# Attention beside an FFT filter: matrix-engine work in longer runs of one tiling mode, two activation sets of two banks, another load order

## The chip, the cores and the metric

The kernel runs on one core of a Trainium2 chip. A core has a matrix engine (TensorE, PE in the profile) that writes into PSUM, eight banks of 128 partitions by 512 f32; a scalar engine (ACT), a vector engine (DVE) and GpSimd (POOL) that work on SBUF (ACT and DVE read PSUM too); and SyncE (SP), which here issues the DMA transfers. Each engine takes its own instructions in program order and waits on semaphores. The metric is the device time of one execution in microseconds; less is better.

## The reference

Two independent parts share the output, side by side.

```python
def _A_ref(x, w_r, w_i):              # x: 1 x 2048 x 640
    X = rfft2(x.astype(float32))      # over rows and columns
    X = X * (w_r + 1j * w_i)          # 2048 x 321 weights
    return irfft2(X, s=(2048, 640)).astype(bfloat16)

def _B_ref(x, wqkv, wo):              # x: 1 x 2048 x 640, 32 heads of 20
    qkv = (x @ wqkv).reshape(B, S, 3, 32, 20).transpose(2, 0, 3, 1, 4)
    q, k, v = qkv
    p = softmax(einsum("bhqd,bhkd->bhqk", q, k) * 20 ** -0.5)
    o = einsum("bhqk,bhkd->bhqd", p, v)
    return o.transpose(0, 2, 1, 3).reshape(B, S, 640) @ wo

return concatenate([a, b], axis=-1)   # 1 x 2048 x 1280 bfloat16
```

Part B is called the attention here, part A the filter.

## The kernel before, in words

**Attention.** The 32 heads are stored four to a group `g` (eight groups), each head in its own 32 partitions of `KT` and `QT`. A unit is one block of 512 queries and one group; there are 32 units. A unit has 64 score tiles: 16 blocks of 128 keys times 4 heads `j`. A score tile is one matmul of 32 rows by 128 columns with 512 moving columns into one PSUM bank (`score_mm`, L751). Matmuls of different `j` use different rows of the array and run beside each other; those of one such bundle are called a wave here. For the exponential a tile takes one of two ways. On ACT, L1247 makes the exponential of a set of banks: sets of three banks (0, 1, 2) and of two banks (3, 4) by turns, into rings of three buffers each. On DVE, one tile at a time goes from a bank to int16 (L875), and for four tiles together three operations (L903, L904, L905) make two f16 parts whose products are summed. The products with V are matmuls of 128 rows by 32 columns (L982, `try_pv`), one per ACT tile and two per DVE tile, of which four with different `j` can form a wave; they accumulate over a unit in one bank. A unit ends with a copy (L1003), four f32 matmuls that put queries into rows (L1015), a reciprocal and a product (L1022, L1028). When a query block has all eight groups, `jobs_out` transposes (L1050) and multiplies with `wo` (L1065).

**Full-array work.** All else on PE uses the array as 128 by 128: transposes of `x` (L533), the projections of the first two groups straight into place (`proj0`, L555), packed projections of the others (L581) whose rows DMAs on the chip then spread to the heads' partitions (`spread_heads`), V (L627), and the filter's four stages (L1464, L1515, L1601, L1627). The filter's input is folded on POOL (L1437 to L1445) after both halves were loaded into a zone that held `x`; its tables are loaded between stages into zones that earlier stages have left. Banks 5, 6 and 7 are shared by DVE tiles, V products and full-array work.

**Who sets the order.** A planner in the program (`run`, `step_pe`) simulates the engines with a table of durations and writes down each engine's instructions in the order in which it took them; `add` and `plan` then put in the semaphore waits. So the order is fixed when the program is built. On PE it takes, when free: a fill of an ACT set with score tiles (with at most one DVE tile beside it), else a DVE tile, else a wave of V products, else full-array work whose release time (`rel`, spread evenly over `FT0` to `FT1` for the filter) has come. SP takes the first DMA of its list whose inputs are there.

**The start.** SP loads `x` for the attention, then 16 narrow slices of `wqkv` for the first two groups (`pad_w`), then twelve broadcasts of constant rows into the spare partitions of `KT` and `QT` (`constR`), then the three thirds of `wqkv`.

## Time and profile before

| | |
|---|---|
| runs | 1002.26, 992.9, 996.78 us; median 996.78 us |
| profiled execution | 998.17 us; span of its instructions 996.4 us |
| mean granted TensorE clock | 0.944 of full |
| PE busy | 931.4 us, 93% |
| ACT busy | 792.8 us, 80% |
| DVE busy | 706.5 us, 71% |
| POOL busy | 84.6 us, 8% |
| ACT exponentials (L1247) | 331 of three banks, 335 of two, 3 of one |
| DVE tiles (L875) | 382 |

Busy shares are averages over the span. PE's matmuls overlap, so that a busy PE need not be one at its peak: what a matmul costs in a stream is read from the distance between starts, not from its own duration. The granted clock is given for each stretch of time; at 0.50 a matmul takes twice as long.

### The profile page before, as it was taken

Reading aid. Unit: us, or ns where it says so; the run is one execution under the profiler, and the core shown is the slowest. Engines: PE = TensorE matmul, PEld = TensorE weight load, DVE = VectorE, ACT = ScalarE, POOL = GpSimd, SP = SyncE. Lnnn points to the kernel's source line nnn. Section 1 sums busy time; section 2 is a strip of 40 time slices with the busy share of each in tenths; the row PEclk is TensorE's granted clock in tenths of the full one; section 3 lists DMA queues with packets and bytes.
Section 4 is the critical chain, followed back from the end, with each engine's and each line's share of the span. In section 5 each row is a group of like instructions: output and inputs, shape, how many; then the busy total and the mean of one; then the engine's idle time right before and its main releaser. Section 6 shows DMA issues by size and latency. Waiting matters only on the chain.

```text
span 996.4 us, 14901 instructions
## 1 busy us (share of the span) xinstructions
PE 931.4 (93%) x6322; PEld 321.6 (32%) x6372; DVE 706.5 (71%) x1082; ACT 792.8 (80%) x679; POOL 84.6 (8%) x93
## 2 busy tenths in 40 slices
PE   7479999999889999999999999999999999999997
PEld 3133422434222333223223333332333332333333
DVE  4427566687886877778737788785777776778874
ACT  3258487988875889889979898997888988888882
POOL 1000000000399100000020020100000000000000
PEclk9789999999765999999979999997999999999999
DMA  7940201110500001100110100011001000010001
GB/s 145 95 125 5 48 22 43 22 22 22 190 1 1 21 7 43 43 2 1 47 27 8 34 20 21 21 43 43 23 21 43 20 8 1 1 49 19 27 28 55
DMA packets 29697, 35.33 MB, mean 35 GB/s; under 512 B 13240, under 2 KB 26298, under 8 KB 28602
## 3 DMA queue, kind: packets, MB, share of 16 engines
q1 hardware_dynamic: 28858, 33.02, 13.2%
q0 software_dynamic: 768, 1.32, 0.5%
q8 instruction: 51, 0.84, 0.3%
q14 instruction: 20, 0.16, 0.1%
HBM read 24.66 MB, written 5.24 MB: 30 GB/s over the span
## 4 chain that ended last, share of the span: by engine, by line
PE 81%; DVE 9%; DMA 4%; ACT 2%; SPq 2%; issue 1%
PE ps L751 26%; PE ps L982 26%; PE ps L1601 5%; PE ps L1015 4%; PE ps L1464 4%; PE ps L581 4%; DVE arena L875 4%; DMA arena<-in_B_wqkv_dram 4%; PE ps L1627 3%; PE ps L1515 3%; PE ps L1065 3%; ACT arena L1247 2%; PE ps L627 2%; DVE arena L904 2%; SPq L421 2%
## 5 line engine op out<-in xcount | busy, mean ns | idle before, releaser
L1247 ACT ACTIVATE arena<-ps 128x1024 f16<-128x1024 f32 (+1 forms) x669 | 785.6, 1233 | 171.3 <-PE ps L751 139.6
L875 DVE TENSOR_SCALAR arena<-ps 128x512 int16<-128x512 f32 x382 | 260.2, 689 | 187.2 <-PE ps L751 184.3
L751 PE MATMUL ps<-arena 32*128 32x512 bf16 x2048 | 345.9, 399 | 15.5 <-ACT arena L1247 8.2
L982 PE MATMUL ps<-arena 128*32 128x512 f16 x2430 | 348.5, 404 | 7.2 <-DVE arena L904 3.3
L751 PEld LDWEIGHTS ps<-arena 32*128 32x128 bf16 x2048 | 81.8, 91 | 249.4 <-issue 133.5
L982 PEld LDWEIGHTS ps<-arena 128*32 128x32 bf16 x2430 | 81.1, 94 | 205.7 <-issue 174.6
L904 DVE TENSOR_TENSOR arena<-arena 128x2048 f16<-128x2048 f16 (+1 forms) x97 | 121.6, 1254 | 2.3
L903 DVE TENSOR_SCALAR arena<-arena 128x2048 uint16<-128x2048 uint16 (+1 forms) x97 | 69.4, 715 | 2.3
L905 DVE TENSOR_SCALAR arena<-arena 128x2048 uint16<-128x2048 uint16 (+1 forms) x97 | 66.9, 690 | 0.3
L1601 PE MATMUL ps<-arena 128*128 128x512 bf16 (+1 forms) x176 | 56.1, 394 | 1.3 <-issue 1.3
L1015 PE MATMUL ps<-arena 128*128 128x85 f32 x256 | 51.8, 315 | 1.5 <-DVE arena L1003 1.2
L627 PE MATMUL ps<-arena 128*128 128x160 bf16 x320 | 31.6, 240 | 20.9 <-DMA arena<-in_B_wqkv_dram 20.8
L581 PE MATMUL ps<-arena 128*128 128x512 bf16 x164 | 47.3, 383 | 2.4 <-issue 1.3
L1015 PEld LDWEIGHTS ps<-arena 128*128 128x128 f32 x256 | 38.2, 205 | 25.8 <-issue 16.1
L1464 PE MATMUL ps<-arena 128*128 128x512 bf16 x144 | 44.3, 384 | 2.0 <-issue 1.8
L1515 PE MATMUL ps<-arena 128*128 128x322 bf16 (+1 forms) x198 | 40.3, 309 | 2.0 <-DVE arena L875 0.6
L633 DVE CAST arena<-ps 128x320 bf16<-128x320 f32 x32 | 15.7, 492 | 34.3 <-PE ps L627 34.1
L1627 PE MATMUL ps<-arena 128*128 128x320 bf16 (+1 forms) x192 | 36.6, 302 | 0.6 <-DVE arena L875 0.2
L588 DVE TENSOR_SCALAR arena<-ps 128x512 bf16<-128x512 f32 x36 | 24.8, 689 | 16.5 <-PE ps L581 15.3
L1437 POOL TENSOR_TENSOR arena<-arena 128x640 f32<-128x640 bf16 x8 | 12.9, 1606 | 261.8 <-DMA arena<-in_A_x_dram 261.3
L1065 PE MATMUL ps<-arena 128*128 128x320 bf16 x160 | 32.1, 312 | 1.6 <-DMA out_dram<-arena 1.2
L627 PEld LDWEIGHTS ps<-arena 128*128 128x128 bf16 x320 | 22.2, 100 | 32.9 <-issue 30.4
(60 smaller groups left out, 399.7 us busy)
## 6 DMA issues: line engine op xcount, KB each, us to landing
arena<-ct SPq DMA_DIRECT2D x8, 1024.0 KB
out_dram<-arena SPq DMA_DIRECT2D x32, 160.0 KB
arena<-arena SPq DMA_DIRECT2D x42, 80.0 KB
arena<-in_A_x_dram SPq DMA_DIRECT2D x2, 1280.0 KB
arena<-in_B_wqkv_dram SPq DMA_DIRECT2D x3, 800.0 KB
arena<-constR SPq DMA_DIRECT2D x8, 288.0 KB
arena<-in_B_x_dram SPq DMA_DIRECT2D x3, 640.0 KB
arena<-cFD SPq DMA_DIRECT2D x1, 966.0 KB
```

What stands on the lines that cost most here:

```text
L581: return lambda e: e.matmul(o, l, r_, start=(cc == 0), stop=(cc == 4))
L627: return lambda e: e.matmul(o, l, r_, start=st, stop=(c == 4), skip_group_check=True)
L751: return e.matmul(self.ps[:, bank, :], self.KT[32 * j:32 * j + 32, g, kt * 128:(kt + 1) * 128], self.QT[32 * j:32 * j + 32, g, qc * 512:(q ...
L875: return e.tensor_scalar(o, in_, 0.0, 31744.0, ALU.max, ALU.min)
L903: (lambda e, en: e.tensor_scalar(Gu, Iu, 0x3FF, 0x3800, ALU.bitwise_and, ALU.bitwise_or), 70 + 0.26 * 512 * n, ik, [("G", b), ("G2", b)], ...
L904: (lambda e, en: e.tensor_tensor(Gf, If, Gf, ALU.mult), 70 + 0.52 * 512 * n, ik + [("G", b)], [("G2", b)], [], "p3"),
L982: inst = e.matmul(self.ps[32 * j:32 * j + 32, bank, :], v_, p_, start=s_, stop=False, tile_position=(0, 32 * j), skip_group_check=True)
L1015: return lambda e: e.matmul(o, l, self.sel, start=(qt == 0), stop=(qt == 3), skip_group_check=True)
L1247: self.put("act", lambda e: e.activation(o, in_, AF.Exp, bias=ACT_BIAS, scale=ACT_SCALE), 0.8333 * 512 * n + 95.0, r=[("ps", b) for b in b ...
L1464: return lambda e: e.matmul(o, l, r_, start=(t == 0), stop=(t == 7))
L1515: return lambda e: e.matmul(o, lhs, r_, start=st, stop=sp)
L1601: return lambda e: e.matmul(o, l, r_, start=(n == 0), stop=(n == 7))
```

## The change

- **Fewer, longer runs on PE.** The planner charges `SW` for each step between score matmuls ("S"), V products ("V") and full-array work ("B"). V products are taken when eight are ready (`VMIN`), up to four waves in one go, each wave made of different `j` (`pv_waves`). Work other than a fill is taken only as far as it fits before the next fill is due (`room`). A fill of an ACT set can bring up to two DVE tiles with it, all of different `j`; DVE tiles have no other way in.
- **Banks.** ACT sets are banks 0, 1 and 2, 3; banks 4 to 7 are shared. The exponentials go into one ring of seven buffers of two tiles. Up to three DVE tiles may be under way (two before), none before a planned time of 30 us.
- **Order of units.** `UNITS` takes query blocks 0 and 1 of groups 0 to 3 by turns, then the rest. `proj0` makes a second query block.
- **Loads.** The narrow slices are gone: two slices of 160 columns are loaded and four copies on DVE pad them. The constant rows are gone: 14 memsets on POOL fill `KT` and `QT`, and the spread transfers then overwrite the heads' rows. V's third of `wqkv` is loaded after the first half of `x`.
- **Fold.** The filter's input is loaded in rows of 128 right after the transposes of `x`, folded on POOL as before, stored to a scratch in DRAM, and loaded folded when the filter begins.
- The planner's durations and latencies have new values, and the last output copies may run on ACT.

The core of the diff:

```diff
+UNITS = ([(qc, g) for g in range(4) for qc in range(2)] + [(0, g) for g in range(4, 8)] + [(1, g) for g in range(4, 8)]
+         + [(qc, g) for qc in range(2, 4) for g in range(8)])
...
-    L_PE = 150.0
-    L_ACT = 120.0
...
+    L_PE = 215.0
+    L_ACT = 165.0
...
+    SW = 102.0
+    FILL = 445.0
+    SETS = ((0, 1), (2, 3))
+    POOLB = (4, 5, 6, 7)
+    RING = (7,)
...
+        self.dma(self.ident, cBd.ap()[:, 0:128], 32768, w=[("ident",)], name="ld_id")
+        for t in range(2):
+            self.dma(self.xn[0][:, 2 * t:2 * t + 2, :], xB[:, 2 * t:2 * t + 2, :], 327680, w=[("xn", 0, 2 * t), ("xn", 0, 2 * t + 1)], name="ld_x0")
+        for c0, nm in ((640, "wk0"), (0, "wq0")):
+            self.dma(self.wqkv[:, :, c0:c0 + 160], wv[:, :, c0:c0 + 160], 204800, w=[(nm,)], name="ld_" + nm)
...
+        def ld_x(i):
+            self.dma(self.xn[i], xB[:, 4 * i:4 * i + 4, :], 655360, w=[("xn", i, t) for t in range(4)], name="ld_x%d" % i)
+        ld_x(1)
+        self.dma(self.wqkv[:, :, 1280:1920], wv[:, :, 1280:1920], 819200, w=[("wv",)], name="ld_wv")
+        ld_x(2)
+        ld_x(3)
+        self.dma(self.wqkv[:, :, 800:1280], wv[:, :, 800:1280], 614400, w=[("wk",)], name="ld_wk")
...
-        crk = cRd.ap()[0:12, :].rearrange("p (g s) -> p g s", g=1).to_broadcast([12, 6, 2048])
-        crq = cRd.ap()[12:24, :].rearrange("p (g s) -> p g s", g=1).to_broadcast([12, 6, 2048])
...
-            p0, p1 = 32 * j + 20, 32 * j + 32
-            self.dma(self.KT[p0:p1, 2:8, :], crk, 294912, w=[("KTc", j)], name="ld_kc", rel=6000.0)
-            self.dma(self.QT[p0:p1, 2:8, :], crq, 294912, w=[("QTc", j)], name="ld_qc", rel=6000.0)
...
+                d_ = self.w0[g][i].rearrange("p c (j e) -> p c j e", e=32)[:, :, :, 0:20]
+                s_ = self.wqkv[:, :, 640 * i + 80 * g: 640 * i + 80 * g + 80].rearrange("p c (j e) -> p c j e", e=20)
+                self.dve_push([((lambda d_, s_: lambda e, en: e.tensor_copy(d_, s_))(d_, s_), 420.0, [("w0z",), (("wq0", "wk0")[i],)], [("w0", g, i)], [], "padw")],
...
+        for g in range(2, 8):
+            self.pool_op((lambda v: lambda e: e.memset(v, one2))(self.KT[:, g, :].bitcast(F32)), 1000.0, w=[("KTm", g)], name="ms_k")
+            self.pool_op((lambda v: lambda e: e.memset(v, off2))(self.QT[:, g, :].bitcast(F32)), 1000.0, w=[("QTm", g)], name="ms_q")
...
-        if self.dve_wants():
+        dts = []
+        while len(tiles) + len(dts) < 4 and self.dve_wants(len(dts)):
             db = self.free_bank()
+            if db is None:
+                break
+            dt = self.pick_dve_tile(set(t[2] for t in tiles), dts)
+            if dt is None:
+                break
+            dts.append((dt, db))
+            self.dve_take(dt, db)
...
+            for wv in waves:
+                if all(x["tile"][2] != j for x in wv):
+                    wv.append(it)
+                    break
+            else:
+                waves.append([it])
+        return waves, sum(len(w) for w in waves)
...
+        for i, wv in enumerate(waves):
+            if i >= nmax or (i > 0 and len(wv) < 3 and not flush):
                 break
-            group.append(it)
...
+        nxt = sum(self.exp_occ(len(t[0])) for t in self.sets)
+        limit = max(self.free["act"], self.now) + nxt - self.FILL - self.SW
...
+        press = self.pv_pressure() or limit > self.now + 1e8
+        if nv >= self.VMIN or (nv and (press or fin)):
+            k = max(1, int((room - self.SW) // 216.0))
+            if self.try_pv(k, flush=press or fin):
...
+    VMIN = 8
+    PRP = 1
+    EARLY = 30000.0
...
+        for t in range(8):
+            f = t % 3
+            xa, xb = self.fx[f][:, 0:640], self.fx[f][:, 640:1280]
+            for i, x_ in enumerate((xa, xb)):
+                r0 = 1024 * i + 128 * t
+                self.dma(x_, xA[r0:r0 + 128, :], 163840, r=[("xs", i, t - 3)] if t >= 3 else [], w=[("fx", f, i), ("fxl", t, i)], name="ld_fx")
...
+                self.dma(self.xs[i][128 * t:128 * t + 128, :], dst, 163840, r=[("ff", t, i, q) for q in range(3)] + [("fx", f, i)], w=[("xs", i, t)], name="st_fx")
...
         def load_x():
             for i in range(2):
-                src = xA[1024 * i:1024 * i + 1024, :]
-                self.dma(self.xf[i], src.rearrange("(t p) d -> p t d", p=128), 1310720, w=[("xf", i), zr("A", 0)], name="ld_xA")
...
+                self.dma(self.xf[i], self.xs[i].rearrange("(t p) d -> p t d", p=128), 1310720, r=[("xs", i, t) for t in range(8)], w=[("xf", i), zr("A", 0)], name="ld_xA")
...
```

In PE's order, in the filter's third stage (the tiles of unit 22), with L751 and L776 the score matmuls, L982 and L1016 the V products, L1601 and L1688 the filter's and L1048 the end of a unit; before:

```order
L751 MATMUL ps<-arena 128x512 x4
L982 MATMUL ps<-arena 32x512 x3
L1601 MATMUL ps<-arena 65x512
L751 MATMUL ps<-arena 128x512 x2
L982 MATMUL ps<-arena 32x512 x2
L751 MATMUL ps<-arena 128x512
L1601 MATMUL ps<-arena 65x512 x3
L751 MATMUL ps<-arena 128x512 x3
L982 MATMUL ps<-arena 32x512 x3
L1601 MATMUL ps<-arena 65x512 x2
```

And at the same place now:

```order
L776 MATMUL ps<-arena 128x512 x3
L1688 MATMUL ps<-arena 128x512 x2
L776 MATMUL ps<-arena 128x512 x2
L1016 MATMUL ps<-arena 32x512 x8
L776 MATMUL ps<-arena 128x512 x3
L1688 MATMUL ps<-arena 128x512
L1048 MATMUL ps<-arena 128x85
L776 MATMUL ps<-arena 128x512 x2
L1016 MATMUL ps<-arena 32x512 x8
```

The fills keep their number; the V products no longer follow nearly every fill in twos and threes but every second one in eights, and full-array work stands between the others. Over the whole order, up to the fallback that is normally skipped, there are 799 runs of score matmuls before and 806 now, 726 and 344 of V products, 562 and 511 of full-array work; steps from one mode to another: 2,086 and 1,660.

In SP's order at the start of the program, where `in_B_x_dram` is `x`, `in_B_wqkv_dram` the weights and `constR` the constant rows; before:

```order
L421 DMA arena<-in_B_x_dram 128x640 x4
L421 DMA arena<-constI 128x128
L421 DMA arena<-constF 128x85
L421 DMA arena<-constF 128x3
L421 DMA arena<-in_B_x_dram 128x4x640 x3
L421 DMA arena<-in_B_wqkv_dram 128x5x20 x16
L421 DMA arena<-constR 12x6x2048 x2
```

And now:

```order
L440 DMA arena<-constI 128x128
L440 DMA arena<-in_B_x_dram 128x2x640 x2
L440 DMA arena<-in_B_wqkv_dram 128x5x160 x2
L440 DMA arena<-constF 128x3
L440 DMA arena<-in_B_x_dram 128x4x640
L440 DMA arena<-in_B_wqkv_dram 128x5x640
L440 DMA arena<-in_B_x_dram 128x4x640 x2
L440 DMA arena<-in_B_wqkv_dram 128x5x480 x2
```

The wide slice of the weights, V's, is the eighth transfer now; before, the first wide slice stands behind the 16 narrow ones and all twelve of `constR`.

More of the change, by code (lines that the diff above doesn't have):

```diff
@@ L404, in put_dma @@
     def put_dma(self, fn, nbytes, r=(), w=(), pw=(), name="dma", stream=None, out=False):
+        rate = 90.0 if name == "spread" else 270.0
         if stream is None:
@@ L591, in jobs_B @@
         sb = 0
-        U0, UL = 16000.0, 23000.0
-        need = [2, 2, 3, 4, 6]
         hist = []
-        for c in range(5):
-            for which in (1, 0):
-                if which == 1 and c == 0:
-                    continue
+        order = [(1, 1), (0, 1), (1, 2), (0, 2), (1, 3), (0, 3), (1, 4), (0, 4), (0, 0)]
+        for n_, (which, c) in enumerate(order):
                 js = []
@@ L1153, in try_bg @@
                 continue
-            if not self.ready(J):
+            if min(sum(c[1] for c in J.pe), self.BMIN) + self.SW > room or not self.ready(J):
                 continue
@@ L1199, in want_pv @@
             return False
-        return any(it["tile"][0] == u for it in self.pv)
+        return any(it["tile"][0] == u and self.avail([("V", UNITS[u][1] // 2, it["tile"][1])]) for it in self.pv)
     def pick_dve(self, en="dve"):
@@ L1276 @@
-    DVE_LOW = 500.0
-    def P_wait_fill(self):
-        return False
+        nxt = sum(self.exp_occ(len(t[0])) for t in self.sets)
+        limit = max(self.free["act"], self.now) + nxt - self.FILL - self.SW
+        if not self.act_started or self.ua >= NU or not self.pick_set(1):
+            limit = self.now + 1e9
+        fin = self.ua >= NU and not self.sets
+        u = self.upv
+        nv = self.pv_waves(u)[1] if u < NU else 0
+        room = limit - self.now
+        if self.mode == "B" and self.bg_continue(room):
+            return True
@@ L1281, in flush_batch @@
+    BMIN = 300.0
     def flush_batch(self):
```

363 lines of the change are left out of this document (197 added, 166 removed).

## The prediction

> **What bounds the kernel now.** I read first the head of the page and the chain of waits.
>
> ```profile
> span 996.4 us, 14901 instructions
> PE 931.4 (93%) x6322; PEld 321.6 (32%) x6372; DVE 706.5 (71%) x1082; ACT 792.8 (80%) x679; POOL 84.6 (8%) x93
> ...
> PE 81%; DVE 9%; DMA 4%; ACT 2%; SPq 2%; issue 1%
> ```
>
> PE carries the chain. Next the busy time by stretches (columns: length, then busy time and instructions of PE, weight loads, DVE, ACT, POOL, then granted clock, DMA share, GB/s).
>
> ```profile
> 5.00:10.00 5.00, 4.89 (x43) 2.95 (x42) 0.89 (x2) 1.24 (x2) 0.00 (x0) 1.00 0.99 317
> 20.00:60.00 40.00, 17.52 (x101) 7.11 (x102) 15.84 (x24) 8.51 (x8) 0.00 (x0) 0.70 0.91 127
> 264.00:330.00 66.00, 60.46 (x310) 16.68 (x306) 48.90 (x58) 43.55 (x37) 61.86 (x64) 0.59 0.05 19
> 330.00:490.00 160.00, 157.26 (x1067) 50.08 (x1082) 122.94 (x183) 141.56 (x122) 0.31 (x2) 1.00 0.05 17
> 490.00:520.00 30.00, 26.80 (x156) 7.39 (x155) 17.30 (x25) 23.41 (x21) 5.36 (x9) 0.72 0.20 61
> 670.00:690.00 20.00, 19.15 (x102) 5.67 (x103) 11.93 (x18) 13.99 (x13) 0.00 (x0) 0.66 0.20 72
> ```
>
> The steady state is 330 to 490: PE 98% busy, ACT 88%, DVE 77%, full clock. Three other stretches have a clock of 0.59 to 0.72, and between 20 and 60 us hardly anything runs. What PE's time consists of is seen in its timeline (start, duration, count; here starts count).
>
> ```profile
> 483.22 1.04 PE L1464 MATMUL ps<-arena 128*128 128x512 bf16 x4
> 484.19 0.39 PE L751 MATMUL ps<-arena 32*128 32x512 bf16 x3
> 484.51 0.40 PE L982 MATMUL ps<-arena 128*32 128x512 f16 x3
> 484.84 0.39 PE L1464 MATMUL ps<-arena 128*128 128x512 bf16 x1
> 485.16 0.40 PE L982 MATMUL ps<-arena 128*32 128x512 f16 x4
> 485.49 0.39 PE L751 MATMUL ps<-arena 32*128 32x512 bf16 x3
> 485.81 0.61 PE L982 MATMUL ps<-arena 128*32 128x512 f16 x6
> 486.35 0.39 PE L1464 MATMUL ps<-arena 128*128 128x512 bf16 x1
> 486.68 0.41 PE L751 MATMUL ps<-arena 32*128 32x512 bf16 x4
> ```
>
> Four full-array matmuls hold PE for 0.97 us, one for 0.32: 0.215 each and 0.105 on top when the next is of another mode. A wave of three or four small ones also costs 0.32, two waves in a row 0.54. So a wave is 0.215 us and a change of mode 0.105.
>
> **PE's part of the change.** Waves before come from the busy time of the two groups, a lone wave counting 0.39 us.
>
> ```profile
> L982 PE MATMUL ps<-arena 128*32 128x512 f16 x2430 | 348.5, 404 | 7.2 <-DVE arena L904 3.3 <-DVE arena L905 2.5 <-DVE arena L1003 0.6
> L751 PE MATMUL ps<-arena 32*128 32x512 bf16 x2048 | 345.9, 399 | 15.5 <-ACT arena L1247 8.2 <-issue 2.0 <-DMA arena<-arena 2.0
> ```
>
> That is 694.4 / 0.39 = 1,780 waves. In the new order there are 825 score waves and 638 waves of V products, if every run is cut into fours (all of one wave have different `j`); up to 50 more if some hold three. Saved: 317 waves x 0.215 = 68 us (57 with 50 more). Changes of mode fall from 2,086 to 1,660: 426 x 0.105 = 45 us. The fills' runs (799 and 806) stay, so all of it comes from the V products and from fewer pieces of full-array work, whose matmuls are the same but for ten more projections. Together 113 us (102 to 113), 3.5 us for each of 32 units of 64 tiles. In the steady stretch ACT made 61 pairs of sets, 305 tiles, and DVE 80 (its row stands below): 385 tiles in 160 us, 26.6 us a unit. Were PE alone the bound, that would become 23.1.
>
> **ACT takes over.** The new order has 831 exponentials of two banks and one of one. Their price back to back:
>
> ```profile
> 59.49 6.88 ACT L1247 ACTIVATE arena<-ps 128x1536 f16<-128x1536 f32 x6 [27.89 <-PE ps L982]
> 970.12 2.37 ACT L1247 ACTIVATE arena<-ps 128x1536 f16<-128x1536 f32 x2 [0.50 <-PE ps L751]
> ...
> L1247 ACT ACTIVATE arena<-ps 128x1024 f16<-128x1024 f32 x335 | 342.2, 1022 | 28.3 <-PE ps L751 27.9
> ```
>
> A pair takes 2.37, its second exponential 1.02, so the first holds ACT for 1.35. Six take 6.88 = 3 x 1.35 + 2 x p + 1.02, so p = 0.905 us for two banks. A unit needs 26 of them, 23.5 us; before, the same tiles in threes and twos cost as much, (1.35 + 0.905) / 5 = 0.451 a tile against 0.4525. So the new sets win nothing on ACT, and ACT (23.5) and PE (23.1) become equal bounds, with DVE at 122.94 / 385 x 64 = 20.4. Two bounds of one size joined by two sets of buffers don't both run full. I take 0.96 us an exponential, ACT 94% busy: between p = 0.915 (99%) and 1.03 (88%, ACT's share now).
>
> [...]
>
> **The start.**
>
> ```profile
> 5.60 13.55 SPq L421 DMA_DIRECT2D arena<-in_B_wqkv_dram  x16
> 19.20 5.03 SPq L421 DMA_DIRECT2D arena<-constR  x12
> ...
> 8.22 4.92 PE L533 MATMUL ps<-arena 128*128 128x128 bf16 x70
> ...
> 56.39 2.69 PE L627 MATMUL ps<-arena 128*128 128x160 bf16 x19 [20.76 <-DMA arena<-in_B_wqkv_dram]
> ```
>
> V's weights land at 56 us, behind 16 narrow slices and twelve broadcasts at 127 GB/s; ACT makes 8 exponentials by then and waits 27.89 us (row at 59.49). Both kinds of transfer go. Ahead of V's weights now lie 0.03 + 0.66 + 0.41 + 0.66 MB and they are 0.82 themselves: 2.6 MB at the 317 GB/s of the wide rows, 8.2 us from about 2 us on, so they land by 10 to 12 us. `x` arrives as before, at 8.22; then transposes (2 us), ten projection matmuls (2.2), a copy, V's first matmuls, a fill: first exponential at 14.5 us (13 to 18). What replaces the transfers, four copies on DVE and 14 memsets on POOL, hides: POOL has nothing else to do then, and its memsets are first needed by the spread for unit 4, two units of work later. In the first unit transposes, projections and copies share PE, DVE and ACT: 5 us more (0 to 10).
>
> **Fold and clock.** With the fold on POOL, DVE's 16-bit operations were slower; rows of 264 to 330 first, then of 330 to 490:
>
> ```profile
> L904 DVE TENSOR_TENSOR arena<-arena 128x2048 f16<-128x2048 f16 x7 | 13.2, 1891 | 0.1
> L903 DVE TENSOR_SCALAR arena<-arena 128x2048 uint16<-128x2048 uint16 x7 | 8.2, 1173 | 0.2
> L905 DVE TENSOR_SCALAR arena<-arena 128x2048 uint16<-128x2048 uint16 x7 | 6.5, 932 | 0.0
> ...
> L875 DVE TENSOR_SCALAR arena<-ps 128x512 int16<-128x512 f32 x80 | 54.8, 689 | 34.5 <-PE ps L751 33.9
> L904 DVE TENSOR_TENSOR arena<-arena 128x2048 f16<-128x2048 f16 x19 | 23.2, 1220 | 0.4
> L905 DVE TENSOR_SCALAR arena<-arena 128x2048 uint16<-128x2048 uint16 x20 | 13.6, 679 | 0.0
> L903 DVE TENSOR_SCALAR arena<-arena 128x2048 uint16<-128x2048 uint16 x19 | 13.1, 691 | 0.5
> ```
>
> That is 1.4 us for a batch of four tiles. The fold's 62 us now lie beside the projections, where DVE also empties their banks (six or seven at 0.69 us a unit): seven batches, 10 us, of which I count 6 (0 to 10). Its 16 loads and 16 stores of 160 KB stand on SP, and spreads behind stores that wait for POOL; but spread heads are first needed by unit 4, at some 119 us (14.5 + 5 + 4 x 25), and the fold, from about 25 us on, ends some 25 us before that.
>
> Clock 0.59 at 264 to 330 while PE is 92% busy: what is missing there is full-array work. PE's groups at 264 to 290:
>
> ```profile
> L982 PE MATMUL ps<-arena 128*32 128x512 f16 x64 | 12.3, 560 | 1.2 <-DVE arena L904 1.1
> L751 PE MATMUL ps<-arena 32*128 32x512 bf16 x53 | 11.7, 538 | 0.6 <-ACT arena L1247 0.6
> L1015 PE MATMUL ps<-arena 128*128 128x85 f32 x8 | 2.9, 465 | 0.0
> ```
>
> In the old order 127 tiles pass there without any but the units' own ends, and 39 and 31 tiles at the two later stretches. The new order has such gaps of 46, 26, 33 and 31 tiles, 10 to 18 us each at 0.39 us a tile. At 264 to 330 ACT made 37 exponentials instead of 50 (0.76 a us at 330 to 490), 17 us lost. For four short gaps I take 10 us (0 to 18).
>
> [...]
>
> **The end.** The last exponential in ACT's timeline, and the row of the waits on which ACT's idle time rests:
>
> ```profile
> 978.30 0.60 ACT L1247 ACTIVATE arena<-ps 128x512 f16<-128x512 f32 x1 [0.35 <-PE ps L751]
> ...
> ACT arena L1247 <- PE ps L751: 139.6, 248, 12.7
> ```
>
> From the last exponential to the end pass 18.1 us. The new order leaves 56 instead of 15 matmuls of the last filter stage behind the last fill: 41 x 0.135 (320 columns at the rate of 512) = 5.5 us. So 23.6.
>
> **Sum.** 14.5 + 5 + 831.5 x 0.96 (798) + 6 + 10 + 23.6 = 857 us of span; the profiled execution has 998.17 - 996.4 = 1.8 us around it: 859. That execution lies 1.4 us over the median, which I leave out.
>
> **Rivals.**
> - *Everything clean*: ACT at 0.915, no halved clock, no loss to the fold: 14.5 + 761 + 22 + 2 = 800. For it: the planner keeps room for fills. Against: PE needs 98% of that pitch. 0.15 for under 830.
> - *Coupled engines*: ACT stays at 88%, 1.03 us: 58 us more, 917. For it: a run of eight V products waits on DVE's batch, and the next fill is queued behind it on PE; four banks must serve DVE tiles, V products and full-array work; and if a third of the eights need three waves, PE is at 23.8. Against: ACT's idle time now comes where PE is full (139.6 us of waits on score matmuls, with PE at 98%). 0.20 for 890 to 950.
> - *Slower: the clock.* As ACT becomes the bound, PE rests a little in every period, and the clock is halved not only in the gaps. A unit then needs 2 x 23.1 = 46 us instead of 25, 21 more; the kernel is slower than 1,007 us once (1,007 - 859) / 21 = 7 of 32 units run so. For it: 264 to 330 shows that a busy PE can be halved. Against: there full-array work was missing, while nearly every unit of the new order has some, at a higher rate per us. [...] 0.04, with 0.03 for 950 to 1,007.
> - *The change doesn't do what it says*: the order shows that it does for V products, and hardly for fills; this is in the sum.
>
> **Chances.** The forecast, 830 to 890, has 0.58. The range 810 to 930 leaves out some 0.05 of the clean case, 0.05 of the coupled one and 0.07 above. About 1% is what a measurement of this kernel can tell from no change: faster by more 0.94, within 0.02, slower 0.04.
>
> **What would show it.** Right: first exponential before 18 us; ACT over 90% busy from 50 us to the end and its pitch under 1.0; runs of eight V products in 0.54 us; a unit in 24 to 26 us; clock below 1 only in the gaps named. Wrong: ACT waiting for PE where PE waits for DVE's batches (the coupled case), or a clock below 0.9 beside full-array work. If the first exponentials wait for spread heads at unit 4, the start was costed wrongly.

## The result and the profile after

The kernel after takes 837.21 us (median of four runs, 831.29 to 841.89) against 995.52 us for the kernel before: a ratio of 0.8398, with a 95% interval from 0.833 to 0.8466. The forecast was 859 us, in a range from 810 to 930. The profiled execution of after took 841.89 us, 1.8 us more than its span. Where a median and a ratio below don't fit together, the ratio is the one to read: it leaves out disturbed runs.

The page of after (head, busy time, granted clock in 40 slices, chain of waits, two of the costliest groups):

```profile
span 840.1 us, 15160 instructions
...
PE 813.8 (97%) x6381; PEld 278.0 (33%) x6381; DVE 686.3 (82%) x1088; ACT 777.9 (93%) x845; POOL 95.7 (11%) x107
...
PEclk9589999999999689999999999999999999979999
...
ACT 52%; PE 42%; DVE 5%; issue 0%
...
L1278 ACT ACTIVATE arena<-ps 128x1024 f16<-128x1024 f32 x832 | 770.2, 1093 | 35.5 <-PE ps L776 25.1
...
L1016 PE MATMUL ps<-arena 128*32 128x512 f16 x2433 | 213.4, 401 | 1.6 <-DVE arena L656 1.6
```

ACT carries half of the chain now, where PE had 81%. The V products (L1016) keep PE busy for 213.4 us instead of 348.5, with nearly the same number of matmuls (2,433 and 2,430). PE is at 97% and ACT at 93%: two bounds of nearly one size. The waits say the same. PE's weight loads for scores wait for ACT, and ACT's own waits for scores fell from 139.6 to 25.1 us (waiting place, what it waited for, total, times, longest):

```profile
PEld ps L776 <- ACT arena L1278: 274.2, 674, 1.4
...
ACT arena L1278 <- PE ps L776: 25.1, 40, 2.0
```

By stretches (same columns as in the prediction):

```profile
16.00:45.00 29.00, 26.69 (x161) 10.67 (x161) 9.07 (x17) 18.52 (x20) 11.44 (x15) 0.59 0.21 70
...
130.00:275.00 145.00, 142.48 (x1201) 48.68 (x1198) 122.72 (x193) 144.19 (x158) 0.00 (x0) 1.00 0.11 23
275.00:300.00 25.00, 23.40 (x136) 5.95 (x134) 16.50 (x25) 19.16 (x20) 0.00 (x0) 0.59 0.56 198
...
575.00:740.00 165.00, 164.42 (x1302) 51.20 (x1305) 143.18 (x221) 164.85 (x181) 0.00 (x0) 1.00 0.05 18
740.00:765.00 25.00, 23.30 (x154) 7.12 (x147) 18.33 (x29) 20.19 (x22) 0.00 (x0) 0.73 0.11 40
...
819.00:840.10 21.10, 16.73 (x137) 11.41 (x131) 12.48 (x31) 3.84 (x8) 0.00 (x0) 1.00 0.24 82
```

Where the clock is full, ACT is idle for 0.15 us of 165: 181 exponentials, 0.912 us each. Three stretches run at half clock for most of their length, and the first of them, 16 to 45 us, was in no term of the prediction. How it begins (timeline: start, duration, count, and the idle time ahead):

```profile
15.54 1.02 ACT L1278 ACTIVATE arena<-ps 128x1024 f16<-128x1024 f32 x1 [1.45 <-PE ps L776]
...
16.67 0.39 PE L776 MATMUL ps<-arena 32*128 32x512 bf16 x4 [0.85 <-DVE arena L582]
18.18 0.39 PE L776 MATMUL ps<-arena 32*128 32x512 bf16 x2 [1.11 <-ACT arena L1278]
19.09 0.61 PE L776 MATMUL ps<-arena 32*128 32x512 bf16 x2 [0.53 <-ACT arena L1278]
```

From 16 to 19 us PE has only pairs of score matmuls and waits for ACT between them. `x` isn't what is missing: by the updates of their semaphores in the trace its last two parts landed by 13.8 and 15.5 us, and their transposes, from 20.18 us on, show no wait for a DMA. The planner's order put them there; an order with the transposes ahead wasn't run. At 19.09 a pair takes 0.61 us instead of 0.39: the clock has halved (0.50 from 18.5 us on), and full-array work that comes back from 20 us on doesn't restore it before 42 us.

An account of PE helps with all that follows. A span is PE's idle time (span less busy time), plus the part of the busy time that the halved clock took (span x (1 - mean granted clock); in after, full-array matmuls of 512 columns in a row start 0.40 to 0.43 us apart at half clock, and 0.22 to 0.23 at full clock), plus the rest, PE's work at full clock. In four of the traces 46 to 63 matmul records are missing (there are more weight loads than matmuls); they are counted as work at the mean busy time of a matmul, 0.15 us or less, 6 to 8 us in all.

| kernel, profiled execution | span | PE's work at full clock | lost to the clock | PE idle | last exponential ends |
|---|---|---|---|---|---|
| before | 996.4 | 883.0 | 55.8 | 57.6 | 978.9 |
| after | 840.1 | 777.7 | 36.1 | 26.3 | 819.8 |
| V products ungrouped | 1003.7 | 897.6 | 28.1 | 78.0 | 825.0 |
| one wave at a time | 876.3 | 804.5 | 44.7 | 27.1 | 833.1 |
| sets of 3 and 2, start mended | 872.8 | 732.2 | 69.8 | 70.8 | 853.3 |
| before, grouped alone | 912.5 | 738.6 | 76.7 | 97.2 | 892.6 |
| fills at the start | 830.3 | 782.1 | 21.6 | 26.6 | 812.1 |
| fills in every gap | 843.8 | 808.1 | 10.1 | 25.6 | 802.3 |
| fills in the longest gaps | 820.7 | 787.1 | 8.2 | 25.4 | 800.3 |
| runs of 12 V products | 847.0 | 775.1 | 33.0 | 38.9 | 827.3 |

From before to after: 105 us less work, 31 us less idle time (20 of it in the first 60 us), 20 us less lost to the clock; together 156 us.

### The profile page after: what moved, and what is told of

It is laid out like the page before. It is cut to its first block, busy times and chain, and to the rows that moved or that the text cites. A ratio compares the mean times of both kernels' runs of the same rounds, so it can differ in the third digit from the quotient of the medians.

```text
span 840.1 us, 15160 instructions
## 1 busy us (share of the span) xinstructions
PE 813.8 (97%) x6381; PEld 278.0 (33%) x6381; DVE 686.3 (82%) x1088; ACT 777.9 (93%) x845; POOL 95.7 (11%) x107
## 4 chain that ended last, share of the span: by engine, by line
ACT 52%; PE 42%; DVE 5%; issue 0%
ACT arena L1278 52%; PE ps L776 14%; PE ps L1016 10%; PE ps L1714 3%; PE ps L1551 3%; PE ps L603 3%; PE ps L650 2%; PE ps L574 2%; PE ps L1048 2%; PE ps L1099 1%; DVE arena L901 1%; DVE arena L930 1%; PE ps L1602 1%; PE ps L1688 1%; PE ps L552 1%; PE ps L532 1%
## 5 line engine op out<-in xcount | busy, mean ns | idle before, releaser
L1278 ACT ACTIVATE arena<-ps 128x1024 f16<-128x1024 f32 x832 | 770.2, 1093 | 35.5 <-PE ps L776 25.1
L776 PE MATMUL ps<-arena 32*128 32x512 bf16 x2048 | 335.0, 396 | 17.3 <-ACT arena L1278 13.1
L1016 PE MATMUL ps<-arena 128*32 128x512 f16 x2433 | 213.4, 401 | 1.6 <-DVE arena L656 1.6
L776 PEld LDWEIGHTS ps<-arena 32*128 32x128 bf16 x2048 | 80.2, 91 | 314.4 <-ACT arena L1278 274.2
L1016 PEld LDWEIGHTS ps<-arena 128*32 128x32 bf16 x2433 | 44.3, 95 | 88.4 <-issue 74.6
L1688 PE MATMUL ps<-arena 128*128 128x512 bf16 (+1 forms) x192 | 57.3, 387 | 0.0
L603 PE MATMUL ps<-arena 128*128 128x512 bf16 x180 | 52.6, 384 | 0.1
L1551 PE MATMUL ps<-arena 128*128 128x512 bf16 x160 | 48.0, 394 | 0.1
L1048 PE MATMUL ps<-arena 128*128 128x85 f32 x256 | 44.0, 297 | 0.0
L1048 PEld LDWEIGHTS ps<-arena 128*128 128x128 f32 x256 | 35.2, 198 | 14.0 <-issue 11.2
L1602 PE MATMUL ps<-arena 128*128 128x322 bf16 (+1 forms) x198 | 37.7, 303 | 0.3
L1633 DVE TENSOR_TENSOR arena<-ps,arena 128x644 bf16<-128x644 f32 (+1 forms) x34 | 28.0, 824 | 3.0 <-PE ps L1602 2.6
L1099 PE MATMUL ps<-arena 128*128 128x320 bf16 x160 | 28.6, 301 | 0.0
```

Of the source, the lines that this page charges most:

```text
L603: return lambda e: e.matmul(o, l, r_, start=(cc == 0), stop=(cc == 4))
L776: return e.matmul(self.ps[:, bank, :], self.KT[32 * j:32 * j + 32, g, kt * 128:(kt + 1) * 128], self.QT[32 * j:32 * j + 32, g, qc * 512:(q ...
L1016: inst = e.matmul(self.ps[32 * j:32 * j + 32, bank, :], v_, p_, start=s_, stop=False, tile_position=(0, 32 * j), skip_group_check=True)
L1048: return lambda e: e.matmul(o, l, self.sel, start=(qt == 0), stop=(qt == 3), skip_group_check=True)
L1278: self.put("act", lambda e: e.activation(o, in_, AF.Exp, bias=ACT_BIAS, scale=ACT_SCALE), 0.8333 * 512 * n + 60.0, r=[("ps", b) for b in b ...
L1551: return lambda e: e.matmul(o, l, r_, start=(t == 0), stop=(t == 7))
```

## Experiments

The theory: PE's sum of waves and mode changes was the bound, and grouping is the gain. The rivals: the new banks, the loads and unit order, or the place of the fold carry it; and the clock decides more than the prediction gave it. All ratios are to the kernel before, with 95% intervals; after's is 0.8398, and 0.8385 (0.8354 to 0.8417) when it was run again.

### Grouping undone

```diff
-        waves, _ = self.pv_waves(u)
...
-        for i, wv in enumerate(waves):
-            if i >= nmax or (i > 0 and len(wv) < 3 and not flush):
+        for it in self.pv:
+            if it["tile"][0] != u or it["tile"][2] in used:
+                continue
...
+            if len(group) == 4:
...
-    VMIN = 8
+    VMIN = 1
-    VLOW = 6
+    VLOW = 1
```

> The kernel after, with only the grouping of V products undone: a wave of them is issued as soon as one product is ready. By the order of the instructions that makes 1,002 V waves instead of 638 and 1,982 changes of mode instead of 1,660, 11 score waves fewer, and 811 exponentials instead of 831. At the prediction's prices 353 x 0.215 + 322 x 0.105 = 110 us more work for PE, about the 113 us that the prediction says the change saved. Theory A (PE's waves and mode changes were the bound and are the gain): PE is the bound again at about 26.6 us a unit, the exponentials' mean pitch rises from 0.967 to 1.05 to 1.10 us, and the time is 905 to 945 us. Rival B (the banks, the loads and the order of the units carry the gain, PE has slack): within 15 us of 837. In both, stretches of 25 to 57 tiles without full-array work become frequent; if they cost the clock, up to 20 us come on top, and the granted clock shows it.

Measured: 1002.76 us, ratio 1.0031 (0.9997 to 1.0065). The whole gain is gone, with the new banks, loads, unit order and fold all in place. Theory A's mechanism holds, its number doesn't: it is 58 to 98 us short. The account gives 120 us more work at full clock (110 expected). But the pitch that A expected at 1.05 to 1.10 us is 0.993 by the starts of the exponentials. What raises it are four waits of 7 to 15 us between 127 and 315 us, 44 us in all, in which PE runs projections and V one after another and ACT has no scores. Outside them the pitch is 0.94, less than after's 0.967, so the last exponential ends at 825 us, hardly later than in after (819.8). What PE could not do was left behind the attention (ACT's wait for scores; two stretches; then PE's timeline in the second):

```profile
ACT arena L1290 <- PE ps L776: 60.0, 21, 15.1
...
45.00:824.00 779.00, 750.93 (x5350) 244.41 (x5348) 635.82 (x959) 721.12 (x787) 46.13 (x47) 0.99 0.07 22
824.00:1003.70 179.70, 134.41 (x752) 73.35 (x750) 96.91 (x166) 4.08 (x8) 18.42 (x23) 0.90 0.23 74
...
857.36 5.49 PE L1614 MATMUL ps<-arena 128*128 128x322 bf16 x24 [4.76 <-DMA arena<-cFD]
873.14 8.60 PE L1614 MATMUL ps<-arena 128*128 128x322 bf16 x42 [10.29 <-DVE arena L1645]
```

The planner fills ACT's banks first, then V products, then full-array work. With more V work it is the filter that falls behind: 180 us of it stand alone at the end (21 in after), and there PE waits for tables and evictions that attention would have hidden, 45 us idle. So most of PE's excess is paid at the end, and with a surcharge. The edit also gives a wave its old price in the planner's table (288 ns for four products instead of 225), which has a part in the order; but PE is idle for only 28 us from 45 to 824 us, so no more than that of the tail can come of it. The frequent stretches without full-array work did not cost the clock: 28 us are lost, less than in after, so such a stretch alone doesn't decide it.

### One wave at a time

```diff
-            if self.try_pv(k, flush=press or fin):
+            if self.try_pv(1, flush=press or fin):
...
-    VMIN = 8
+    VMIN = 3
-    VLOW = 6
+    VLOW = 3
```

> The kernel after, with V products grouped into full waves as before this edit but one wave at a time instead of two or more in a row: 1,866 changes of mode instead of 1,660, 652 V waves instead of 638, 835 exponentials instead of 831. By the prediction's prices 206 x 0.105 + 19 x 0.215 = 26 us more for PE. Theory A with PE 0.4 us a unit under ACT: half of it shows, 842 to 860 us. Rival B (ACT alone is the bound now): 837 within 6 us. Rival C (a mode change costs more than 0.105 us where it stands between ACT's two sets): over 865 us.

Measured: 876.57 us, ratio 0.876 (0.8686 to 0.8834), 4.3% over after. That is in rival C's range, but not by C's reason: the account gives 27 us more work at full clock where the prices gave 26, so a mode change costs what the prediction said. What was wrong is A's hope that half of it would hide beside ACT. The pitch hardly moves (0.976 against 0.967), and the end grows from 21.1 to 43.8 us:

```profile
45.00:832.50 787.50, 770.84 (x5841) 254.83 (x5838) 636.50 (x982) 754.48 (x819) 68.43 (x73) 0.96 0.11 33
832.50:876.30 43.80, 37.62 (x283) 25.89 (x279) 29.74 (x64) 3.71 (x8) 0.00 (x0) 1.00 0.29 100
```

27 us of work and 9 more lost to the clock make up the 36 us of difference. After has no PE slack to give.

### The old banks

```diff
-    SETS = ((0, 1), (2, 3))
-    POOLB = (4, 5, 6, 7)
-    RING = (7,)
+    SETS = ((0, 1, 2), (3, 4))
+    POOLB = (5, 6, 7)
+    RING = (3, 3)
```

> The kernel after, with only the old division of the banks: ACT's sets of three and two banks, three shared banks. Its order has 349 exponentials of three banks and 359 of two (102 tiles more on ACT, as DVE gets fewer), 1,323 changes of mode and 700 + 640 waves: 62 us less for PE than after. Theory A (engines' sums are the bound, the banks only divide the work): ACT is the bound at 349 x 1.35 + 359 x 0.905 = 796 us, 44 more than after's 752, so 865 to 890 us. Rival B (the old division is what kept ACT waiting in before, where a pair of sets took 2.82 us): 349 x 2.82 and 37 around it, 1,000 to 1,030 us. Rival C (PE is still the bound, and its 62 us count): under 837 us.

Measured: 906.21 us, ratio 0.9068 (0.9 to 0.9137), above A's range. The start spoilt it: the planner let projections hold a bank of the first set until all were done.

```profile
56.77 0.85 PE L650 MATMUL ps<-arena 128*128 128x160 bf16 x10
58.15 0.61 PE L776 MATMUL ps<-arena 32*128 32x512 bf16 x7 [0.52 <-ACT arena L656]
```

So it was run again with the start mended:

```diff
-        banks = self.POOLB if self.act_started else (0, 1, 2, 3, 4, 5, 6, 7)
+        banks = self.POOLB if self.act_started else (3, 4, 5, 6, 7)
```

> The old division of the banks again (sets of three and two, three shared), with the start mended: in the first run of it all projections were planned ahead of the first score matmul, which came at 58 us instead of 15, since background work held the first set's banks. Here background work keeps out of them. 357 exponentials of three banks and 358 of two, 1,787 tiles on ACT (1,663 in after), 712 + 635 waves, 1,448 changes of mode. Theory A (ACT's sum is the bound, at the pitches of the first run of it, 1.371 and 0.957): 489 + 343 = 832 us, with 16 ahead and 21 behind: 865 to 875 us, so the division of the banks is worth some 30 us, all of it tiles that DVE takes from ACT. Rival B (the 43 us of late start were not on the path, since PE did projections then): 890 to 910 us. Rival C (PE is the bound, its work is 44 us less than after's): under 845 us.

Measured: 867.92 us, ratio 0.8691 (0.8666 to 0.8716): theory A's 865 to 875. PE has 46 us less to do than in after and is idle for 71; ACT's sum is longer (busy time of the two groups):

```profile
L1278 ACT ACTIVATE arena<-ps 128x1536 f16<-128x1536 f32 x357 | 545.7, 1529 | 13.5 <-PE ps L776 11.7 <-PE ps L1016 0.4
L1278 ACT ACTIVATE arena<-ps 128x1024 f16<-128x1024 f32 x358 | 396.2, 1108 | 11.4 <-PE ps L776 7.2 <-PE ps L1016 3.8
```

The new division is worth 3.5%, some 30 us, and not by cheaper exponentials. With it DVE takes 124 tiles more (1,663 of 2,048 are on ACT instead of 1,787): PE pays with waves and mode changes, ACT gains. Whether the fourth shared bank does it, or the smaller sets, beside which a fill can bring two DVE tiles and not one, isn't shown. The mended start has a part in the 30 us: the first unit ran at full clock and took 30.9 us, against 43.2 in after, so the rest of the run loses more than 30.

### Grouping alone, on the kernel before

```diff
-        if self.dve_wants() and self.dve_backlog() < self.DVE_LOW and not self.want_pv():
...
-        if self.try_pv():
-            return True
-        if self.try_bg():
+        if self.mode == "B" and self.bg_continue(room):
+            return True
...
+        if nv >= self.VMIN or (nv and (press or fin)):
+            k = max(1, int((room - self.SW) // 216.0))
+            if self.try_pv(k, flush=press or fin):
+                return True
+        if self.bg_resume(room):
+            return True
+        if self.try_bg(room):
```

The rest of `try_pv`, `pv_waves`, `bg_continue` and `bg_resume` is that of after.

> The kernel before with the grouping alone: score matmuls, V products and full-array work are chosen as in the kernel after (eight V products at a time, a piece of full-array work only where it fits before ACT's next fill), while the loads, the start, the order of the units, the place of the fold and the banks (sets of three and two, three shared) stay as in before. By its order 693 + 679 waves instead of 815 + 871 and 1,454 changes of mode instead of 2,086: at the prediction's prices 314 x 0.215 + 632 x 0.105 = 134 us less for PE. Theory A (PE's sum is the bound of before and the grouping is the gain): at least 100 of the 134 us show, until ACT binds: 338 x 1.37 + 352 x 0.96 = 801 us of exponentials, some 45 of start and 23 of end, 870; so 865 to 900 us. Rival B (the parts only work together: the grouping alone runs into the old start, the old fold and long gaps): 930 to 990 us.

Measured: 914.31 us, ratio 0.9176 (0.9136 to 0.9215), between A and B. PE's work fell by 144 us (134 expected), but only 82 us show. Idle time rose by 40 us and the loss to the clock by 21: the old start stands (the first unit of 64 tiles takes 55 us, PE busy for half of it beside a DMA share of 0.69). In it ACT waits 31.2 us for V products, which wait for V, whose weights PE waits for (25.4 us).

```profile
22.00:77.00 55.00, 28.31 (x233) 12.48 (x233) 19.66 (x30) 23.35 (x21) 0.00 (x0) 0.75 0.69 106
...
ACT arena L1259 <- PE ps L999: 34.9, 6, 31.2
...
L636 PE MATMUL ps<-arena 128*128 128x160 bf16 x320 | 31.1, 245 | 25.9 <-DMA arena<-in_B_wqkv_dram 25.4
```

With the run that undoes the grouping of V products: the planner's choice of after alone is half of the gain, and all else without grouping is none of it. The parts don't add up, since each only moves the bound as far as the next one.

### The fold at its old place

```diff
-                self.dma(self.xf[i], self.xs[i].rearrange("(t p) d -> p t d", p=128), 1310720, r=[("xs", i, t) for t in range(8)], w=[("xf", i), zr("A", 0)], name="ld_xA")
+                src = xA[1024 * i:1024 * i + 1024, :]
+                self.dma(self.xf[i], src.rearrange("(t p) d -> p t d", p=128), 1310720, w=[("xf", i), zr("A", 0)], name="ld_xA")
+            a_, b_ = self.ftmp
+            for t in range(8):
...
```

> The kernel after, with only the input fold at its old place: GpSimd folds in place just before the filter's first stage, and there is no scratch in DRAM. The fold's 62 us on GpSimd then lie beside DVE's 16-bit operations of the middle of the run and not beside the projections, and the filter's work comes later: 167 tiles follow one another without full-array work (46 in after). Theory A (without full-array work the clock halves, at about 5 us per 20 us of half clock as in after's gap): some 65 us at half clock, 11 us more, and 6 us given back in the first stage: 838 to 852 us. Rival B (PE has slack at half clock, and the fold's place doesn't matter): 837 within 5 us. Rival C (half clock makes PE the bound for the whole gap): over 860 us.

Measured: 880.31 us, ratio 0.8736 (0.8649 to 0.8823), 4.0% over after: 34 us. That is the size of rival C. The profiled execution is some 13 us longer than the ratio says, so only its gap is read here:

```profile
270.00:365.00 95.00, 87.16 (x500) 22.17 (x500) 74.55 (x95) 74.26 (x77) 63.63 (x64) 0.55 0.16 56
```

In 95 us at a clock of 0.55 ACT makes 77 exponentials; at after's 0.912 it would make 104. So 25 us are lost here, where after by the same count loses 7 in its own gap (20 exponentials in the 25 us from 275, with GpSimd idle: the fold beside DVE isn't needed for such a loss). The first three units take 86.6 us instead of 93.2, so the 6 us are given back as expected. On balance the early fold, which the prediction counted as a cost alone, is a gain: it lets the filter start early and closes a gap of 167 tiles down to 46. This execution also loses 20 us in its last unit, at half clock, and 13 behind it; how much of that the shorter executions (868 and 878 us) lose isn't known.

### The old unit order

```diff
-UNITS = ([(qc, g) for g in range(4) for qc in range(2)] + ...
+UNITS = [divmod(u, 8) for u in range(32)]
```

> The kernel after, with only the old order of the units: all eight head groups of a query block, then the next block. 807 + 634 waves and 1,590 changes of mode, 12 us less PE work than after. The heads of groups 2 to 7 are then needed for units 2 to 7, not from unit 4 on. Theory A (the projections and spreads come in time): 825 to 838 us. Rival B (scores wait for the spread of heads, as the new order asks for them later): the exponentials' pitch rises in units 2 to 7, by 2 to 6 us a unit: 850 to 875 us.

Measured: 889.32 us, ratio 0.8827 (0.8779 to 0.8875), 5.1% over after: 43 us. Rival B's order of size, above its range. The profiled execution is some 18 us longer than the ratio says. ACT's waits from 16 to 170 us, and a row of PE's timeline in the longest of them:

```profile
ACT arena L1277 <- PE ps L775: 44.1, 23, 16.1
...
92.13 5.70 PE L649 MATMUL ps<-arena 128*128 128x160 bf16 x80
```

In after these waits are 12.7 us. The longest, from 85 to 101 us, lies ahead of the third unit, the first whose heads come by packed projections and spread. Rival B's cause isn't quite what the trace shows: PE waits for no DMA there but is busy with projections and V, which its order has ahead of the next scores. The first four units take 149.6 us instead of 116.7, which is 33 of the 43 us; the rest I can't place, and this execution loses 94 us to the clock where after loses 36. The prediction used the new order only to say that heads are first needed by unit 4; undone, it costs more than the banks.

### Full-array matmuls at the start

```diff
+        self.filler()
...
+    FILL_N, FILL_K = 5, 2
...
+        o, l, m = self.ps[:, b, :], self.KT[:, 0, 0:128], self.QT[:, 0, 0:512]
...
+            for i in range(self.FILL_K):
+                inst = e.matmul(o, l, m, start=True, stop=True)
```

> The kernel after, with ten full-array matmuls (128x512, their result is never read) put between the first score matmuls: two behind each of ACT's second to sixth fill, 2.2 us of PE work in the stretch from 16 to 20 us where the profile of after shows PE with little to do (0.39 us busy of 16 to 18). Nothing of the computation is left out. Theory A (the thin stretch makes the clock halve at 18.5 us, and the 23.9 us at half clock are what made the first unit of 64 tiles take 43 us): full clock through the first unit, which takes 28 to 33 us, and 10 to 14 us less in all: 822 to 828 us. Rival B (the first unit is slow because transposes, projections and V lie in it, and x comes late): half clock gone or not, the first unit stays at 40 us and the time at 837 within 5 us. Rival C (fillers delay the transposes, the clock halves later anyway): 837 to 845 us.

Measured: 834.58 us, ratio 0.8362 (0.8322 to 0.8402). The number is in rival B's range, but what slowed the first unit is shown to be the clock: it stays full through that unit, which takes 30.9 us instead of 43.2, and in 31 us ACT makes 30 exponentials where after made 20 in 29.

```profile
16.00:47.00 31.00, 29.14 (x257) 11.91 (x256) 16.04 (x26) 27.21 (x30) 15.99 (x18) 1.00 0.24 78
...
17.45 13.08 ACT L1297 ACTIVATE arena<-ps 128x1024 f16<-128x1024 f32 x14 [0.54 <-PE ps L777]
```

The saving isn't shown, since its interval overlaps after's. In its own profiled execution 13.7 us from 459 and 20.5 us from 548 ran at half clock, where after's first execution had 6.8 us, and in after's second profiled execution the first stretch at half clock was 10.2 us long instead of 23.9 and the first unit took 33.4. How long the clock stayed halved differed from execution to execution.

### Full-array matmuls in the gaps

```diff
+            if k <= self.FILL_N or self.ua >= NU or self.now - self.last_b < self.FILL_GAP:
+                return
+    FILL_GAP = 2500.0
```

`FILL_GAP` is planned time in ns without full-array work (other than the units' ends); the second of these kernels has 5000.0.

> As the run with ten fillers at the start, and three fillers more behind a fill of ACT's wherever no projection, transpose or filter matmul was planned for 2.5 us: 36 such places, 108 matmuls, 23 us of PE work and up to 72 changes of mode, 8 us. Nothing is left out. Theory A (each stretch without full-array work costs the clock, and the half clock of after's five gaps, 48 us in all, costs a quarter of its length): the granted clock is 1.00 from 20 us on and 12 us are won; PE is a bound beside ACT, so up to 31 us are paid: 820 to 845 us, above the run with fillers at the start alone if PE is full. Rival B (PE has slack, ACT alone is the bound): 5 to 12 us under the run with fillers at the start alone. Rival C (the clock halves for another reason than missing full-array work): half clock stays in the gap after 278 us.

Measured: 848.23 us, ratio 0.8509 (0.8473 to 0.8545). The clock is full but for 17 us from 506 and 3 at the end, also in the gap after 278 us, so rival C is out, and attention ends 18 us earlier than in after; yet the end takes 42.2 us, with a single run of 162 filter matmuls in it:

```profile
46.00:801.60 755.60, 740.92 (x5894) 241.38 (x5893) 643.39 (x991) 740.04 (x802) 67.91 (x71) 0.99 0.11 34
801.60:843.80 42.20, 35.46 (x275) 24.93 (x267) 29.16 (x65) 3.78 (x8) 0.00 (x0) 0.97 0.30 103
...
816.46 22.26 PE L1740 MATMUL ps<-arena 128*128 128x320 bf16 x162
```

Theory A, 3 us beyond its range: 26 us more work than with fills at the start alone, 11 us less lost to the clock, 14 us more in all. So here half clock cost PE's sum, and so did what prevented it.

> The kernel with ten fillers at the start, and three fillers more only where no projection, transpose or filter matmul was planned for 5 us: 6 such places in the whole run, 18 matmuls, 3.9 us of PE work and up to 12 changes of mode. Nothing is left out. Theory A (a few full-array matmuls in the longest gaps hold the clock): the half clock of some 20 to 40 us that the kernel with start fillers still had goes, 5 to 10 us won for 5 paid: 828 to 834 us. Rival B (six bursts are too few, or others halve instead): 834 to 842 us.

Measured: 821.39 us, ratio 0.825 (0.8224 to 0.8276): 1.6% under after in the same set of runs (0.825 / 0.8385 = 0.984, about 0.5% either way with the two intervals added in squares), 7 us better than A's range. Eighteen matmuls in six places cost 5 us of work, as priced, and take the loss to the clock from 22 to 8 us. All five executions have a mean clock of 0.989 to 0.994, the four with fills at the start alone 0.948 to 0.974. What is left is mainly one stretch of 13.7 us at half clock from 269 us; the end stays short:

```profile
47.00:799.10 752.10, 728.41 (x5870) 244.51 (x5929) 649.83 (x1015) 740.32 (x804) 67.00 (x71) 0.99 0.13 38
799.10:820.70 21.60, 16.81 (x141) 11.10 (x133) 12.96 (x31) 4.29 (x8) 0.00 (x0) 0.95 0.23 80
```

This is the fastest kernel of the case.

### Longer runs of V products

```diff
-    VMIN = 8
+    VMIN = 12
-    VLOW = 6
+    VLOW = 12
```

> The kernel with ten fillers at the start, and V products issued twelve at a time instead of eight (307 runs of them instead of 341, 1,630 changes of mode instead of 1,669, the waves and exponentials the same). Theory A (PE's sum is still the bound): 39 x 0.105 = 4 us less, 828 to 833 us. Rival B (longer runs hold back ACT's fills and the seven buffers of exponentials, so ACT waits): 838 to 850 us.

Measured: 848.83 us, ratio 0.8517 (0.8474 to 0.8561): rival B. Against the kernel with fills at the start PE's work fell by 7 us (4 expected), its idle time rose by 12 and the loss to the clock by 11. ACT waits longer for V products to free its buffers (11.0 us with runs of eight) and for scores (14.8):

```profile
ACT arena L1304 <- PE ps L1042: 19.1, 46, 1.8
ACT arena L1304 <- PE ps L779: 18.3, 26, 1.5
```

Of the sizes that were run (one wave, eight, twelve) eight is the best: at twelve, what PE saves ACT loses.

### The kernel after again

> The kernel after once more, beside the three others on the same chip, as their measure: 832 to 842 us by both theories.

Measured: 836.7 us, ratio 0.8385.

## Why the prediction was right, and where it was not

- **PE's sum as the bound, 113 us saved.** Right. The account shows 105 us less work, undoing the grouping brings 120 back where 110 was priced, and one-wave products cost 27 where 26 was priced. What the prediction didn't have is where an excess of PE shows: less in ACT's pitch than behind the attention. Counted from the starts of the matmuls, after has 1,489 waves and 1,660 mode changes: of the "up to 50 more" waves 26 came.
- **The share of the other parts.** The prediction gave the banks, the fold and the unit order nothing or a cost. Undone one at a time they cost some 30, 34 and 43 us. For the banks the step "the new sets win nothing on ACT" is right about an exponential, but it took the number of tiles on ACT as given.
- **ACT's pitch, 0.96 us (0.915 to 1.03).** The mean is 0.967, but that it lies so close is luck. The step said that two equal bounds joined by two sets of buffers don't both run full. They do: 0.912 us over 165 us, ACT 99.9% busy; at that pitch the 831.5 exponentials are 758 us and not 798. The mean is raised by the stretches at half clock and the first unit, which the sum had as terms of their own (10 and 5 us, and 6 for the fold). They were counted twice, and that is most of the 22 us by which the forecast was high.
- **First exponential at 14.5 us.** It started at 15.54.
- **First unit, 5 us more (0 to 10).** Wrong: 43.2 us instead of the 30 of the sum (33.4 in a second execution). The step "transposes, projections and copies share PE, DVE and ACT" isn't what failed: at full clock, with the ten matmuls, the unit takes 30.9. The sum lacked a term for the clock at the start, where ACT made 20 exponentials in 29 us.
- **Fold, 6 us (0 to 10).** The mechanism is there: beside the fold (45 to 95 us) DVE's operation takes 1.9 us, after it 1.2.

```profile
L930 DVE TENSOR_TENSOR arena<-arena 128x2048 f16<-128x2048 f16 x5 | 9.5, 1907 | 0.1
...
L930 DVE TENSOR_TENSOR arena<-arena 128x2048 f16<-128x2048 f16 x18 | 21.9, 1216 | 0.2
```

  The second and third unit took 24.9 and 25.1 us, against 23.1 and 23.9 with the fold at its old place, and the first 43.2 against 39.6. So some 3 to 7 us of it reached the path, one execution of each, and the size fits. The step left out what the fold's old place had cost.
- **Half clock in four gaps, 10 us (0 to 18).** Right in sum: the units at 276 and 740 us took 29.3 and 29.6 us instead of some 24, and of the two other gaps one shows 7 us at half clock and one none.
- **The end, 23.6 us.** 21.1.
- **The rivals.** The clean case has its pitch but not its clock. The coupled case didn't come: ACT waits 9.9 us in all for V products. The slower case happened in one place, a clock of 0.50 beside full-array work from 20 to 42 us, though the prediction counted on full-array work to keep it away; it took one unit and not seven.

## What to carry to other kernels

Where matmuls of several tiling modes interleave, price PE by waves and mode changes (0.215 and 0.105 us here), and look at what stands behind the last work of the other engine: with this planner, which serves ACT first, most of PE's excess showed not in ACT's pitch but as a tail (with the grouping undone 180 us of it instead of 21). Undo the parts of a large change one at a time and also add the main part alone: here undoing it cost the whole gain, while adding it alone brought half. Where a stretch has a granted clock under 1 while PE reads as busy, try a handful of full-array matmuls in its longest gaps and no more, since each is paid out of PE's sum: here 18 of them in six places won 1.6% and 108 in 36 lost.

## What the runs showed of the hardware

The clock was at half for most of a stretch in which PE was over 90% busy (0.59 from 16 to 45 us of after, with PE busy for 26.69 of 29 us). In after the stretches at half clock are 3.4, 6.8, 13.7, 20.5 and 23.9 us long, in before also 17.1 and 34.1: all of them multiples of 3.41, but for the last one of each execution (1.0 and 4.0). I cut the fourteen profiled executions of this case, from 20 us on, into such windows. For each I took the used share of the array from the matmuls that start in it: rows x columns of the tile over 128 x 128, times the columns streamed at 0.42 ns each (512 in the 0.215 us of the prediction). Of 94 windows at full clock with a share under 0.30, 67 were followed by half clock; of 3,033 with more, 28; in the executions of before and after alone it is 7 of 13, and 5 of 459. At half clock the median share is 0.28 in windows that were followed by another halved one, and 0.38 in those followed by full clock. At the start of after the share is 0.19 in the window from 15.1 to 18.5 us, after which the clock halves, 0.30 to 0.40 in the next six, and 0.45 in the one ahead of full clock; with the ten matmuls it is 0.41 at the same place. So PE stayed slow beside full-array work there while the share lay under that 0.45. It is a correlation, and what ends half clock isn't shown by it.

The recorded duration of an exponential of two banks was not its pitch: 1,093 ns on average in after and 1,022 before, while half of after's start at most 904 ns behind the one ahead, and so does the quickest tenth in before. The price had to come from runs of them back to back.
